# One 512-column product in place of two of 256 for the fourth form of a two-level scheme, and one more addition at the output

## The chip, the cores and the metric

The kernel runs on one core of a Trainium2 chip. The core has a matrix engine (TensorE, PE in the profile, with its weight loads as PEld), a vector engine (VectorE, DVE), an activation engine (ScalarE, ACT), GpSimd (POOL) and SyncE (SP), which here issues most of the DMAs. The metric is the device time of one execution in microseconds (us). Before the change the median of three runs is 686.04 us (685.83 to 686.23).

## The reference

An attention with 32 memory slots is followed by a feed-forward block with a gate.

```
a   = softmax(phi)                      # 8 batches, 8 heads, 576 positions, 32 slots
k_m = a^T k ;  v_m = a^T v              # 32 x 64 for each head
attn = softmax(q k_m^T / 8)
x   = (attn v_m), heads side by side    # 4608 x 512
h   = x w_in                            # 512 -> 2048
out = (h * sigmoid(h)) w_out            # 2048 -> 512
```

All arrays are float32.

## The kernel before, in words

The work goes batch by batch. For each batch the attention's probabilities `a` are made transposed, and `v_m` is folded into `w_in`, so that the hidden layer is one product of the probabilities with a projected weight. Numbers are held as a high and a low part in the type `F32R`, and a product of two numbers is three: high with high, high with low, low with high.

Batches 0 and 1 run plainly: 16 hidden chunks of 128 columns, each followed by `ffn2` (L712), which adds 512-column products into four PSUM banks, `acc`. During batch 1 the sums and differences of blocks of `w_out`, the forms of a Strassen-like scheme, are made (`w_forms`, L779) and kept: `kept[3j]`, `kept[3j+1]`, `kept[3j+2]` are the third, fourth and second form of step j. Each kept tile has 512 columns, the high part of the form in the first 256 and its low part in the last 256. `Q` is 256.

Batches 2 to 7 run the scheme. A batch has two halves of 256 main rows, `t` = 0 and 1, and a half has eight steps, `j` = 0 to 7 (`NP` is 8). Slot `s` of a batch issues, in this order: the 12 hidden products of step s (`ffn1s`, L818), the activation and the forms of the hidden values (`forms`, L836: the gate on ACT at L841, sums on DVE at L846, L849 and L850, high parts on ACT at L845 and L855, low parts on DVE at L856 and L857), the attention work planned for this slot, and then `st_step` (L875) for the step before it. `st_step` does seven products of a form of the hidden values with a form of the weights. Each is three products of 256 columns (`product`, L860): `HIGH` is high with high and high with low, `LOW` is low with high. They are added into four PSUM banks, `sums[0]` to `sums[3]`. A bank has 512 columns, and banks 0, 1 and 2 hold two blocks of 256, told apart by `place`. Bank 3 holds one, the fourth form's, in its first 256 columns; the other 256 columns are free. The first product into a bank after a new half begins sets it (`start`), and all later ones add.

In the order of a step, all `HIGH` products come first and then all `LOW` ones; the banks are met in the order 0, 3, 1, 2. The last step of a half mixes the two so that banks 0 and 3 are done early. After it, `st_out` (L896) combines the blocks: ACT copies banks 0 and 1, and the DVE does four additions (L910 to L913, all by the helper at L907): two read bank 2, one reads none, and the fourth subtracts bank 3 into `c21`. Then the stores of `c11` and `c21` are issued on SP (traced as L913 and L914). Three more additions are left to a later slot.

The four banks have one tag, `acc`, with four buffers. A new half's banks are given out by the planner from those that have been released; a bank is released when its last reader is done.

After batches 3, 5 and 7 the 64 leftover rows of two batches follow (`left_st`, L936), in three banks, `lsum`.

The order of PE and ACT instructions in this stage is the order of the program text. That of the DVE and of SP is the planner's, which at each point takes the earliest traced instruction that it finds ready.

Of the kernel before, what the change touches and what calls it, by code (L numbers as in the profile page):

```python
# [16 lines left out]
ALU = mybir.AluOpType  # L17
# [31 lines left out]
def attn_ffn_kernel(  # L49
# [708 lines left out]
    Q = DMODEL // 2  # L758
# [3 lines left out]
    kept, kept_at = [], []  # L762
# [97 lines left out]
    def product(bank, place, part, k, w, first):  # L860
        hi, lo = part
        whi, wlo = w
        for gt, wt in first:
            gt, wt = (hi, lo)[gt], (whi, wlo)[wt]
            key = bank, place
            nc.tensor.matmul(  # L866
                sums[bank][:, place * Q : (place + 1) * Q], gt[:, k], wt,
                start=bank not in begun, stop=True, skip_group_check=True,
            )
            begun.add(bank)  # L870

    sums, begun = [], set()
    HIGH, LOW = ((0, 0), (0, 1)), ((1, 0),)

    def st_step(b, t, j, part):  # L875
        if j == 0:
            sums[:] = [ps.tile([P, DMODEL], F32, tag="acc", name=f"sum{i}", bufs=NI) for i in range(4)]
            begun.clear()
        b11, b12, b21, b22 = (
            (wo_hi[:, 2 * j + k, q * Q : (q + 1) * Q], wo_lo[:, 2 * j + k, q * Q : (q + 1) * Q])  # L880
            for k in range(2) for q in range(2)
        )
        t3, t4, t2 = ((x[:, :Q], x[:, Q:]) for x in kept[3 * j : 3 * j + 3])
        todo = (
            (0, 0, 0, b11), (0, 1, 2, b21), (3, 0, 1, t4), (1, 0, 6, b22), (1, 1, 4, b12), (2, 0, 5, t2), (2, 1, 3, t3)
        )
        order = [(HIGH, todo), (LOW, todo)]
        if j == NP - 1:
            order = [(HIGH, todo[:5]), (LOW, todo[:2]), (HIGH, todo[5:]), (LOW, todo[2:])]
        for terms, some in order:  # L890
            for bank, place, k, w in some:
                product(bank, place, part, k, w, terms)
        if j == NP - 1:
            st_out(b, t)

    def st_out(b, t):  # L896
        o = sb.tile([P, 2, DMODEL], F32, tag="cva", name="oo", bufs=1)
        x = sb.tile([P, 2, Q], F32, tag="cva1", name="x", bufs=1)
        for i in range(2):
            nc.scalar.activation(o[:, i], sums[i], AF.Copy)  # L900
        (c11, c21), (p3, p5) = ((o[:, i, :Q], o[:, i, Q:]) for i in range(2))
        c12, c22 = x[:, 0], x[:, 1]
        r = b * S + 2 * t * P
        one, two = slice(r + P, r + 2 * P), slice(r, r + P)

        def add(to, a, c, op=ALU.add):
            nc.vector.tensor_tensor(to, a, c, op=op)  # L907

        add(c12, sums[2][:, :Q], c11)
        add(c22, sums[2][:, Q:], c12)  # L910
        add(c11, c11, c21)
        add(c21, c22, sums[3][:, :Q], ALU.subtract)
        nc.sync.dma_start(out[one, :Q], c11)  # L913
        nc.sync.dma_start(out[two, :Q], c21)  # L914

        def rest():
            add(c22, c22, p5)
            add(c12, c12, p5)
            add(c12, c12, p3)
            nc.sync.dma_start(out[two, Q:], c22)  # L920
            nc.sync.dma_start(out[one, Q:], c12)

        ev(*((b, 9) if t == 0 else (b, NFC + 1) if b % 2 else (b + 1, 3)), rest)
# [12 lines left out]
    def left_st(b, n, gs):  # L936
        if n == 0:
            sums[:] = [ps.tile([P, DMODEL], F32, tag="acc", name=f"lsum{i}", bufs=NI) for i in range(3)]
            begun.clear()
        part = [x.rearrange("p (n f) -> p n f", f=P) for x in gs]  # L940
        last = n == NLS - 1
        if last:
            o = sb.tile([P, DMODEL], F32, tag="cva", name="ol", bufs=1)
            x = sb.tile([P, Q], F32, tag="cva1", name="xl", bufs=1)
        for bank, (ks, q) in enumerate((((0,), 0), ((1,), 0), ((0, 1), 1))):
            cs = slice(q * Q, (q + 1) * Q)
            for i in range(2):
                for k in ks:
                    fc = 2 * (2 * n + i) + k
                    product(bank, 0, part, 2 * i + k, (wo_hi[:, fc, cs], wo_lo[:, fc, cs]), HIGH + LOW)  # L950
            if not last:
                continue
            if bank == 0:
                nc.scalar.activation(x, sums[0][:, :Q], AF.Copy)
                continue
            nc.vector.tensor_tensor(o[:, cs], sums[bank][:, :Q], x, op=ALU.add)
            for k, r in enumerate((b - 1, b)):
                queue = nc.scalar if b == B - 1 and k else nc.sync
                queue.dma_start(out[r * S + MAIN : r * S + S, cs], o[k * LEFT : (k + 1) * LEFT, cs])
# [3 lines left out]
    def ev(b, slot, fn, *a):  # L963
        events.setdefault((b, slot), []).append((fn, a))
# [40 lines left out]
    for b in range(B):  # L1005
        n = b + 1
# [183 lines left out]
    def finish(tiles):  # L1190
        if prev is None:
            return
        if prev[0] == "main":
            main_step(prev[1], prev[2], prev[3], tiles)
        elif prev[0] == "left" and tiles[0] == 0:
            if prev[1] < 2:
                left_step(prev[1], prev[2], prev[3])
                t1_load(prev[2])
            else:
                left_st(prev[1], prev[2], prev[3])  # L1200
        elif prev[0] == "st" and tiles[0] == 0:
            st_step(*prev[1:])
# [13 lines left out]
    for b in range(B):  # L1216
# [3 lines left out]
        for s in range(NFC if b > 1 else 0):  # L1220
            t, j = divmod(s, NP)
# [5 lines left out]
        for fc in range(NFC if b < 2 else 0):  # L1227
# [7 lines left out]
            for part in range(2):  # L1235
# [3 lines left out]
                n = len(traced)  # L1239
# [78 lines left out]
```

## Time and profile before

| What | Value |
|---|---|
| median of three runs | 686.04 us |
| profiled execution | 685.86 us |
| its span, first to last instruction | 684.0 us |
| PE busy | 673.9 us, 99% |
| PE weight loads busy | 595.7 us, 87% |
| DVE busy | 516.9 us, 76% |
| ACT busy | 368.3 us, 54% |
| products of L866 into `sum`, 256 columns | 2016 |
| granted TensorE clock | 1.000 |

A timeline row of the profile has the start in us from the span's beginning, the time from the first to the last instruction that it merges, the engine, the line, the operation, the tiles written and read, the shape and the count. Matrix products are pipelined: a product starts while the one before it is still on its way, so the busy time of one is a latency, and the distance between two starts is the pace. A weight load (PEld) runs ahead of its own product. In brackets stand the idle time of the engine just ahead, and what ended it.

### The profile page before, as it was taken

To read this page: it belongs to the slowest core of one execution; us is meant where nothing else is said; L and a number is where in the kernel's file an instruction comes from. 1 tells how busy PE (TensorE), PEld (TensorE's weight loads), DVE (VectorE), ACT (ScalarE), POOL (GpSimd) and SP (SyncE) were. 2 spreads that over 40 slices of the span, in tenths; PEclk is the share of its full clock that TensorE was granted. 3 is DMA by queue.
4 is the path that set the end of the run, shared out by engine and by line. 5 is a ranking of instruction groups with operands and counts; after the bars stand their busy time and mean duration, and the time that the engine had idled before them with its cause. 6 is when DMAs were issued, how large, how long until landed. Compare 5 with 4: busy or idle time off the path is not lost.

```text
span 684.0 us, 14812 instructions
## 1 busy us (share of the span) xinstructions
PE 673.9 (99%) x5932; PEld 595.7 (87%) x5932; DVE 516.9 (76%) x1087; ACT 368.3 (54%) x677; POOL 0.7 (0%) x6
## 2 busy tenths in 40 slices
PE   8899999999999999999999999999999999999997
PEld 3578778787889998899998999899989999889997
DVE  4897899988938588868876588886885668767653
ACT  3878684533535455644645546564653636554541
POOL 0000000000000000000000000000000000000000
PEclk9999999999999999999999999999999999999999
DMA  9998975224360562153420434125431204210001
GB/s 345 347 338 275 330 292 203 87 87 161 101 211 3 176 224 100 40 189 133 156 93 17 161 123 177 64 94 183 154 117 40 79 1 155 83 57 17 32 1 47
DMA packets 38228, 93.93 MB, mean 137 GB/s; under 512 B 4752, under 2 KB 22032, under 8 KB 34576
## 3 DMA queue, kind: packets, MB, share of 16 engines
q1 hardware_dynamic: 37136, 90.22, 37.9%
q10 hardware_dynamic: 1024, 2.77, 1.1%
q8 instruction: 47, 0.77, 0.4%
q14 instruction: 21, 0.17, 0.1%
HBM read 77.22 MB, written 15.73 MB: 136 GB/s over the span
## 4 chain that ended last, share of the span: by engine, by line
PE 74%; DVE 7%; ACT 2%; issue 2%; DMA 1%; SPq 1%; DVEq 0%; ACTq 0%
PE sum L866 32%; PE h L827 20%; PE acc L719 6%; PE lsum L866 5%; PE bg L636 3%; PE h L676 3%; PE accleft L719 2%; PE bg L335 1%; DVE pm L654 1%; PE bg L382 1%; DMA fm<-fm 1%; DVE gbuf L846 1%; SPq L88 1%; ACT gbuf L841 1%; DMA qz<-qm 1%
## 5 line engine op out<-in xcount | busy, mean ns | idle before, releaser
L827 PE MATMUL h<-aparts,pm 128*128 128x288 f32 x1152 | 169.1, 296 | 0.2 <-ACT gleft L843 0.2
L827 PEld LDWEIGHTS h<-aparts,pm 128*128 128x128 f32 x1152 | 157.0, 188 | 1.5 <-issue 0.7
L841 ACT ACTIVATE gbuf<-h 128x512 f32<-128x512 f32 x96 | 57.3, 596 | 124.5 <-PE h L827 122.6
L866 PE MATMUL sum<-wo_hi,aparts 128*128 128x256 f32 x384 | 104.0, 293 | 0.0
L866 PE MATMUL sum<-kept,aparts 128*128 128x256 f32 x576 | 100.1, 282 | 0.0
L866 PE MATMUL sum<-wo_lo,aparts 128*128 128x256 f32 x384 | 100.1, 282 | 0.0
L846 DVE TENSOR_TENSOR gbuf<-gbuf 128x256 f32<-128x256 f32 x96 | 40.5, 422 | 78.6 <-ACT gbuf L841 77.9
L866 PEld LDWEIGHTS sum<-wo_hi,aparts 128*128 128x128 f32 x384 | 72.8, 190 | 19.2 <-ACT gleft L843 15.9
L855 ACT ACTIVATE aparts<-gbuf 128x512 fp32r<-128x512 f32 x86 | 54.4, 633 | 64.4 <-DVE gbuf L850 64.4
L719 PE MATMUL acc<-wo_hi,gparts 128*128 128x512 f32 x256 | 85.3, 397 | 0.2
L866 PEld LDWEIGHTS sum<-kept,aparts 128*128 128x128 f32 x576 | 82.6, 191 | 0.0
L857 DVE TENSOR_TENSOR gparts<-gbuf,aparts 128x512 fp32r<-128x512 f32 x86 | 59.4, 690 | 18.5 <-ACT aparts L855 18.5
L866 PE MATMUL sum<-wo_hi,gparts 128*128 128x256 f32 x384 | 73.2, 281 | 0.0
L866 PEld LDWEIGHTS sum<-wo_lo,aparts 128*128 128x128 f32 x384 | 73.1, 190 | 0.0
L866 PE MATMUL sum<-kept,gparts 128*128 128x256 f32 x288 | 65.5, 282 | 0.0
L719 PEld LDWEIGHTS acc<-wo_hi,gparts 128*128 128x128 f32 x256 | 47.5, 188 | 14.5 <-DVE t L809 1.7
L866 PEld LDWEIGHTS sum<-wo_hi,gparts 128*128 128x128 f32 x384 | 59.4, 190 | 0.0
L676 PEld LDWEIGHTS h<-aparts,pm 128*128 128x128 f32 x372 | 51.8, 188 | 6.4 <-issue 1.8
L676 PE MATMUL h<-aparts,pm 128*128 128x288 f32 x372 | 56.0, 299 | 0.4 <-ACT aparts L604 0.4
L845 ACT ACTIVATE aparts<-gbuf 128x384 fp32r<-128x384 f32 x96 | 50.4, 525 | 0.0
L719 PE MATMUL acc<-wo_lo,gparts 128*128 128x512 f32 x128 | 49.4, 394 | 0.2 <-DVE wo_lo L182 0.2
L866 PEld LDWEIGHTS sum<-kept,gparts 128*128 128x128 f32 x288 | 47.9, 190 | 0.0
(206 smaller groups left out, 987.0 us busy)
## 6 DMA issues: line engine op xcount, KB each, us to landing
win<-win_saved SPq DMA_DIRECT2D x24, 1024.0 KB, 4.9
kv<-in_kv SPq DMA_DIRECT2D x28, 516.0 KB, 4.7
q<-in_q SPq DMA_DIRECT2D x16, 576.0 KB, 4.9
raw<-in_w_in SPq DMA_DIRECT2D x14, 512.0 KB, 7.8
raw<-in_w_out SPq DMA_DIRECT2D x6, 1024.0 KB, 5.9
win_saved<-win SPq DMA_DIRECT2D x4, 1024.0 KB, 8.7
phi<-in_phi SPq DMA_DIRECT2D x7, 576.0 KB, 5.9
out<-oo SPq DMA_DIRECT2D x26, 128.0 KB, 1.8
```

The source lines that it names most:

```text
L88: i = (queue or nc.sync).dma_start(dst, src)
L335: nc.tensor.matmul(pt[p][M * r : M * (r + 1), :KVW], e[:, p, c, M * r : M * (r + 1)], kvt[c][:, p, r], start=c == 0, stop=False, skip_grou ...
L636: nc.tensor.matmul(bg[M * r : M * (r + 1), p, :w].rearrange("p (k f) -> p k f", f=P), kvT[D * p : D * (p + 1), 1, r], src[D * p : D * (p + ...
L676: nc.tensor.matmul(h[:, hf, :HALF], wt[:, p, fs], a[:, p, hf * HALF : (hf + 1) * HALF], start=n[hf] == 0, stop=n[hf] == 5, skip_group_chec ...
L719: nc.tensor.matmul(acc[key], gt[:, cs], wt[:, fc], start=fc == 0 and n == 0, stop=fc == NFC - 1 and n == 2)
L827: nc.tensor.matmul(h[:, i, :HALF], wt[:, p, f : f + P], a[:, p], start=n == 0, stop=n == 5)
L841: nc.scalar.activation(gbuf[:, :MAIN].rearrange("p (i f) -> p i f", i=2), h[:, :, :w], AF.Silu)
L845: nc.scalar.activation(hi[:, :3], g[:, 1:4], AF.Copy)
L846: nc.vector.tensor_tensor(g[:, 4:6], g[:, :1].broadcast_to([P, 2, P]), g[:, 1:3], op=ALU.subtract)
L855: nc.scalar.activation(hi[:, 3:], g[:, 4:], AF.Copy)
L857: last_split.append(nc.vector.tensor_tensor(lo[:, 3:], g[:, 4:], hi[:, 3:], op=ALU.subtract))
L866: nc.tensor.matmul(sums[bank][:, place * Q : (place + 1) * Q], gt[:, k], wt, start=bank not in begun, stop=True, skip_group_check=True,)
```

## The change

For the fourth form (bank 3) the two `HIGH` products, with the form's high part and with its low part, become one product with the whole kept tile of 512 columns as its moving operand. It writes all 512 columns of bank 3: the product with the high part into the first 256, as before, and the product with the low part into the last 256. The `LOW` product of this form stays as it was, 256 columns into the first half. The two halves of the bank are added where the half batch ends: `st_out` has a fifth subtraction, which takes the last 256 columns of bank 3 from `c21`, behind the one that takes the first 256. The store of `c21` comes behind it.

```diff
@@ product
         for gt, wt in first:
+            if bank == 3 and (gt, wt) == (0, 1):
+                continue
             gt, wt = (hi, lo)[gt], (whi, wlo)[wt]
-            key = bank, place
+            n = wt.shape[-1]
             nc.tensor.matmul(
-                sums[bank][:, place * Q : (place + 1) * Q], gt[:, k], wt,
+                sums[bank][:, place * Q : place * Q + n], gt[:, k], wt,
                 start=bank not in begun, stop=True, skip_group_check=True,
             )
@@ st_step
             for bank, place, k, w in some:
+                if bank == 3 and terms is HIGH:
+                    w = (kept[3 * j + 1], None)
                 product(bank, place, part, k, w, terms)
@@ st_out
         add(c21, c22, sums[3][:, :Q], ALU.subtract)
+        add(c21, c21, sums[3][:, Q:], ALU.subtract)
         nc.sync.dma_start(out[one, :Q], c11)
```

## The prediction

> **What bounds the kernel now.** I read the page's busy shares first, then the chain that ended last, then a table by stages, and then the instructions in order of time around the lines that the change touches.
>
> ```profile
> span 684.0 us, 14812 instructions
> PE 673.9 (99%) x5932; PEld 595.7 (87%) x5932; DVE 516.9 (76%) x1087; ACT 368.3 (54%) x677; POOL 0.7 (0%) x6
> ...
> PE 74%; DVE 7%; ACT 2%; issue 2%; DMA 1%; SPq 1%; DVEq 0%; ACTq 0%
> PE sum L866 32%; PE h L827 20%; PE acc L719 6%; PE lsum L866 5%; PE bg L636 3%; PE h L676 3%; PE accleft L719 2%; PE bg L335 1%; DVE pm L654 1%; PE bg L382 1%; DMA fm<-fm 1%; DVE gbuf L846 1%; SPq L88 1%; ACT gbuf L841 1%; DMA qz<-qm 1%
> ```
>
> TensorE (PE) is busy 99% of the span, and the products of the changed function, PE sum L866, are alone 32% of the chain. The stage in which they run goes from about 204 us to the end, for batches 2 to 7:
>
> ```profile
> 204.00:684.00 480.00, 475.14 (x4434) 443.69 (x4418) 350.98 (x786) 249.64 (x481) 0.00 (x0) 1.00 0.29 97
> ```
>
> The columns are the stretch, its length, then busy us and count for PE, its weight loads, VectorE (DVE), ScalarE (ACT). PE has 475.14 of 480.00 us filled. So time taken from PE here comes off the end one for one, and so does time that PE is made to wait. A DVE instruction costs something only where PE waits for it.
>
> **The change, part by part.**
>
> *First, two products become one.* Each of the 96 steps (six batches, two halves, eight steps) loses one 256-column product with its weight load, and another grows to 512 columns. A busy time of 282 ns in the profile is a latency, not a pace; the pace is the distance between starts. A step has 21 products and then the 12 of the next hidden step. The rows of one step, with the DVE's and ACT's work beside it, which the second part needs too:
>
> ```profile
> 318.45 1.76 PE L827 MATMUL h<-aparts,pm 128*128 128x288 f32 x12
> ...
> 319.15 0.42 DVE L907 TENSOR_TENSOR x<-sum,oo 128x256 f32<-128x256 f32 x1
> 319.61 0.42 DVE L907 TENSOR_TENSOR x<-sum,x 128x256 f32<-128x256 f32 x1
> ...
> 319.95 0.41 DVE L907 TENSOR_TENSOR oo<-oo 128x256 f32<-128x256 f32 x1
> 320.05 0.28 PE L866 MATMUL sum<-wo_hi,aparts 128*128 128x256 f32 x1
> ...
> 320.24 0.60 ACT L841 ACTIVATE gbuf<-h 128x512 f32<-128x512 f32 x1 [0.76 <-PE h L827]
> ...
> 320.39 0.42 DVE L907 TENSOR_TENSOR oo<-x,sum 128x256 f32<-128x256 f32 x1
> ...
> 320.88 0.42 DVE L846 TENSOR_TENSOR gbuf<-gbuf 128x256 f32<-128x256 f32 x1
> ...
> 321.12 0.55 PEld L866 LDWEIGHTS sum<-kept,aparts 128*128 128x128 f32 x4
> ...
> 321.24 0.64 PE L866 MATMUL sum<-kept,aparts 128*128 128x256 f32 x4
> ...
> 322.54 1.22 PE L827 MATMUL h<-aparts,pm 128*128 128x288 f32 x8
> 322.65 0.69 DVE L857 TENSOR_TENSOR gparts<-gbuf,aparts 128x512 fp32r<-128x512 f32 x1 [0.23 <-ACT aparts L855]
> ```
>
> From 320.05 to 322.54 are 21 products: 2.49 / 21 = 0.1186 us each, so 0.237 for the pair that goes. For 512 columns the trace has the output products of an earlier stage, same type, same 128x128 weights; ten lie between these two starts, and twelve from the second pair on:
>
> ```profile
> 195.20 0.39 PE L719 MATMUL accleft<-wo_lo,gparts 128*128 128x512 f32 x1
> ...
> 197.47 0.40 PE L719 MATMUL accleft<-wo_hi,gparts 128*128 128x512 f32 x1
> ...
> 199.29 0.40 PE L719 MATMUL accleft<-wo_hi,aparts 128*128 128x512 f32 x1
> ...
> 202.05 0.43 PE L827 MATMUL h<-aparts,pm 128*128 128x288 f32 x2
> ```
>
> 2.27 / 10 = 0.227 us, and 2.76 / 12 = 0.230. I take 0.227: each step saves 0.237 - 0.227 = 0.010 us, and 96 of them 1.0 us. Starts are given to 0.01 us, so the difference is good to 0.002: 0.8 to 1.2 us; with 0.230 it is 0.7. The ends are 0.7 and 1.2.
>
> The Trainium skill (TensorE: Matmul & The Clock Gate, Back-to-back issue gap) gives the isolated gap of a warm product as its columns over 2.4 GHz plus about 2.5 ns. By it one product fewer is worth 2.5 ns, an estimate of 0.24 us over 96 steps. It speaks against the change; the same section's 131 ns for 512 columns in a stream speaks wildly for it. The starts above disagree with both (0.1186 and 0.227 us).
>
> *Second, one more subtraction where a half ends.* The new add (128x256, one operand in PSUM) runs 12 times, behind the subtraction that until now was the last reader of bank 3. Its price is that of its neighbours:
>
> ```profile
> L907 DVE TENSOR_TENSOR oo<-x,sum 128x256 f32<-128x256 f32 x12 | 5.0, 418 | 0.3
> ```
>
> That is 12 x 0.42 = 5 us of DVE time, which on its own hides beside PE. What does not hide is the bank. The four banks of a half are handed to the next half's four as they are read out: ACT frees two, then the DVE's second add one, and the subtraction (320.39, ends 320.81) the last. PE uses them in the order bank 0, 3, 1, 2, so the last freed goes to the eleventh product, the t2 form at 321.24 with its weight load at 321.12. That this product waits for that subtraction shows where it comes late:
>
> ```profile
> 443.46 0.28 PE L866 MATMUL sum<-wo_hi,aparts 128*128 128x256 f32 x1
> ...
> 443.67 0.60 ACT L841 ACTIVATE gbuf<-h 128x512 f32<-128x512 f32 x1 [0.94 <-PE h L827]
> ...
> 444.16 0.42 DVE L907 TENSOR_TENSOR oo<-x,sum 128x256 f32<-128x256 f32 x1
> ...
> 444.50 0.42 DVE L846 TENSOR_TENSOR gbuf<-gbuf 128x256 f32<-128x256 f32 x1
> 444.53 0.28 PE L866 MATMUL sum<-wo_lo,aparts 128*128 128x256 f32 x1
> ...
> 444.63 0.54 PEld L866 LDWEIGHTS sum<-kept,aparts 128*128 128x128 f32 x4
> 444.65 0.73 PE L866 MATMUL sum<-kept,aparts 128*128 128x256 f32 x4
> ```
>
> A weight load starts with the product before it; here it should be at 444.53, but it stands at 444.63, 0.05 after the subtraction ended (444.58), and the four products take 0.73 instead of 0.64. So the hand-over costs PE (end of the last read + 0.05) - (planned start of the eleventh product - 0.12), that is, end + 0.17 - planned start, where positive. At 320 us it is 320.81 + 0.17 - 321.24, free by 0.26 us.
>
> The new add needs the subtraction's result. Two dependent adds start 0.46 apart (319.15, 319.61), two independent ones 0.34 (319.61, 319.95). So the last read ends 0.46 later at best: 321.27. PE arrives 0.01 earlier, at 321.23: 321.27 + 0.17 - 321.23 = 0.21 us lost. This form stands at five hand-overs, from first to second half of batches 3 to 7; the last of them has the same 0.43 us between the read's end (639.91) and the product:
>
> ```profile
> 639.49 0.42 DVE L907 TENSOR_TENSOR oo<-x,sum 128x256 f32<-128x256 f32 x1
> ...
> 640.34 0.64 PE L866 MATMUL sum<-kept,aparts 128*128 128x256 f32 x4
> ```
>
> So 5 x 0.21 = 1.05 us.
>
> Four others. At 444 and 606 the DVE comes late from a projection (L654), and L846's input is ready (ACT L841 ends 444.27) while the subtraction runs. L846 is traced earlier than the adds and the DVE's order is the planner's, so I put L846 first, the add 0.34 behind it: start 444.84, end 445.26, + 0.17 - 444.64 = 0.79, less the 0.10 that is lost today: 0.69. At 606 it is 606.10 + 0.34 + 0.42 + 0.17 - 606.34 = 0.69:
>
> ```profile
> 605.76 0.42 DVE L907 TENSOR_TENSOR oo<-x,sum 128x256 f32<-128x256 f32 x1
> ...
> 606.10 0.42 DVE L846 TENSOR_TENSOR gbuf<-gbuf 128x256 f32<-128x256 f32 x1
> ...
> 606.35 0.64 PE L866 MATMUL sum<-kept,aparts 128*128 128x256 f32 x4
> ```
>
> ```profile
> 281.52 0.42 DVE L907 TENSOR_TENSOR oo<-x,sum 128x256 f32<-128x256 f32 x1
> ...
> 282.60 0.64 PE L866 MATMUL sum<-kept,aparts 128*128 128x256 f32 x4
> ```
>
> ```profile
> 243.78 0.41 DVE L907 TENSOR_TENSOR oo<-x,sum 128x256 f32<-128x256 f32 x1
> ...
> 244.12 0.28 DVE L849 TENSOR_TENSOR gbuf<-gbuf 128x128 f32<-128x128 f32 x1
> ...
> 245.00 0.64 PE L866 MATMUL sum<-kept,aparts 128*128 128x256 f32 x4
> ```
>
> At 281 the read ends at 282.40, 0.02 us in time: nothing. At 243 L846 already ran before the subtraction and L849 follows it; with the add behind L849 (244.45, end 244.87) 0.05 us is lost. The remaining three ends (second halves of batches 3, 5, 7) are followed by the leftover rows, which take three banks, those freed earlier: nothing, as the fourth bank is next wanted after four leftover steps. Behind the waiting product, PE's whole queue stands still, 10 more products and the next hidden step; nothing later on PE is free to run past it.
>
> On the DVE, the forms L846 to L857 move by up to 0.42 us. L857 ends 323.34; its result is read by the low products of the next step, which begins 1.60 us after 322.54 (12 hidden products, 318.45 to 320.05) and reads it after 13 to 14 of its own, at about 325.7. More than 2 us of cover is left. The store of the subtracted block leaves 0.46 us later; no row shows a wait on it.
>
> *The sum.* Saved 1.0; lost 1.05 + 0.69 + 0.69 + 0.05 = 2.5; net +1.5 us. The profiled execution took 685.86 us, 1.86 around its span of 684.0, so it would take 687.4. It lies 0.18 below the median of the runs shown, 686.04, on which the forecast is made: **687.5 us**.
>
> **The rivals.**
>
> *The add falls behind L846 at the five regular hand-overs too.* L846 began at 320.88, the add would be free to start at 320.85: a tie, which the planner settles before any run. Then the add runs 321.22 to 321.64, and each of the five loses 0.58: 2.9 + 1.4 + 0.05 - 1.0 = +3.3, 689.3 us. For it speaks the tie and 243 us, where L846 stands ahead of the subtraction; against it that L846 stands behind it at 320, 444 and 606.
>
> *The bank is free in time, and only the saving is left: 685.0 us.* One mechanism: the hand-over. It decides at 321.06 (321.23 - 0.17): if the planner gives the eleventh product a bank whose last read ends before that, or hands the late bank to no product of this step, none of the losses is there. Against it stands the late weight load at 444.63. For it: where slots go is the planner's choice, made with the new add in view.
>
> *The add is paid on the DVE's own path:* up to its 5 us in all, 691 us, if the shifted DVE work stalls the softmax or projections, whose stalls on PE exist today (DVE pm L654 is 1% of the chain). Against it: 2 us of cover above.
>
> *The removed product is worth next to nothing:* if the pace is set by columns alone, the saving is near 0.2 and the sum +2.3, 688.3 us. Against it are the two paces read above. By the skill's isolated gap it would come out so.
>
> **How the numbers follow.** The forecast has 0.45; L846 first 0.25; the saving alone 0.17; the DVE's own path 0.08; the worthless product 0.05. The forecast's own range is 686.9 to 687.9: the saving 0.7 to 1.2, and the adds at 444 and 606 directly behind the subtraction (0.47 each, not 0.69). Both signs hold chances, so the range goes from the saving alone to L846 first: 684.9 to 689.4; beyond it lie half of the saving-alone case and the DVE's path. A measurement tells 0.2%, 1.37 us, from no change: below 684.67 is faster, above 687.41 slower. Faster needs more than the saving's upper end: 0.05, taken from the saving-alone case for what the reads can miss. Same: the rest of that case and somewhat over half of the forecast, which lies on the limit: 0.38. Slower: the others, 0.57.
>
> **What would show it.** The 512-column product should take 0.226 to 0.230 from its start to the next. At the nine hand-overs the weight load of the eleventh product (now the tenth) should stand 0.05 after the new add ends, about 0.2 us late at five places and 0.5 to 0.7 at 444 and 606. Where L846 stands before or behind the add settles the first rival. The prediction is wrong if no weight load is late at those places, if PE's idle time appears elsewhere, or if paces outside the pair move.

## The result and the profile after

The changed kernel takes 687.35 us (median of 12 runs, 686.64 to 689.63); the kernel before, on the same chip, took 685.97 (12 runs). The ratio is 1.0024, with an interval of 1.0016 to 1.0031: slower by 1.4 us. The profiled execution took 687.2 us, with a span of 685.4 (before: 685.86 and 684.0).

From the page of the changed kernel, the span, the busy shares, the chain that ended last by engine and by line, and the two groups of products and weight loads that the change touches (busy us, mean ns of one, idle time ahead). The product's line is now L868, the additions' helper L911:

```profile
span 685.4 us, 14632 instructions
PE 674.6 (98%) x5836; PEld 591.2 (86%) x5836; DVE 520.8 (76%) x1099; ACT 368.2 (54%) x677; POOL 0.7 (0%) x6
...
PE 76%; DVE 7%; ACT 2%; issue 1%; DVEq 0%; ACTq 0%
PE sum L868 33%; PE h L827 20%; PE acc L719 6%; PE lsum L868 5%; PE bg L636 4%; PE h L676 3%; PE accleft L719 2%; PE bg L335 1%; DVE pm L654 1%; PE bg L382 1%; ACT pm L652 1%; DVE gparts L693 0%; ACT gbuf L841 0%; DVE oo L911 0%; DVE gbuf L846 0%
...
L868 PE MATMUL sum<-kept,aparts 128*128 128x256 f32 (+1 forms) x480 | 100.1, 306 | 0.4 <-DVE oo L911 0.4
...
L868 PEld LDWEIGHTS sum<-kept,aparts 128*128 128x128 f32 x480 | 70.7, 189 | 1.5 <-DVE oo L911 1.1
```

96 products are gone and 12 DVE additions have come. What is new is the releaser: products and weight loads of the `kept` forms now wait for `oo L911`, the additions. The 0.4 us in the first group is not what these waits cost. A product's busy time, 0.28 us, covers most of a hole in a stream that should start one every 0.12, so a late product shows as idle only when it is later than that. The loss must be read from starts.

The hand-over at 320 us, in time (start, length, engine, line, operation):

```profile
320.77 0.42 DVE L911 TENSOR_TENSOR oo<-x,sum 128x256 f32<-128x256 f32 x1
...
320.90 0.39 PE L868 MATMUL sum<-kept,aparts 128*128 128x512 f32 x1
...
321.13 0.28 PE L868 MATMUL sum<-wo_hi,aparts 128*128 128x256 f32 x1
...
321.23 0.42 DVE L911 TENSOR_TENSOR oo<-oo,sum 128x256 f32<-128x256 f32 x1
...
321.49 0.28 PE L868 MATMUL sum<-wo_lo,aparts 128*128 128x256 f32 x1
321.57 0.42 DVE L846 TENSOR_TENSOR gbuf<-gbuf 128x256 f32<-128x256 f32 x1
...
321.70 0.53 PEld L868 LDWEIGHTS sum<-kept,aparts 128*128 128x128 f32 x4
321.71 0.74 PE L868 MATMUL sum<-kept,aparts 128*128 128x256 f32 x4
```

The new addition (`oo<-oo,sum`) stands directly behind the subtraction, 0.46 us later, and ahead of L846. It ends at 321.65; 0.05 later the weight load of the tenth product starts. That product should have started at 321.61 (0.12 behind the one at 321.49) and starts at 321.71, and the four take 0.74 instead of 0.64: 0.20 us in all. The 512-column product goes 0.23 us to the next start.

The same at 444 and at 606 us, where the DVE comes late from a projection:

```profile
444.76 0.42 DVE L911 TENSOR_TENSOR oo<-oo,sum 128x256 f32<-128x256 f32 x1
444.77 0.28 PE L868 MATMUL sum<-wo_lo,aparts 128*128 128x256 f32 x1
445.10 0.42 DVE L846 TENSOR_TENSOR gbuf<-gbuf 128x256 f32<-128x256 f32 x1
...
445.23 0.53 PEld L868 LDWEIGHTS sum<-kept,aparts 128*128 128x128 f32 x4 [0.39 <-DVE oo L911]
445.23 0.62 PE L868 MATMUL sum<-kept,aparts 128*128 128x256 f32 x3 [0.18 <-DVE oo L911]
```

```profile
607.06 0.42 DVE L911 TENSOR_TENSOR oo<-oo,sum 128x256 f32<-128x256 f32 x1
607.07 0.28 PE L868 MATMUL sum<-wo_lo,aparts 128*128 128x256 f32 x1
...
607.53 0.74 PE L868 MATMUL sum<-kept,aparts 128*128 128x256 f32 x4 [0.18 <-DVE oo L911]
```

Here too the addition is ahead of L846 (at 606 us that one starts at 607.39), and the wait is long enough to be seen as idle time: 0.34 us from the planned 444.89 to 445.23, and 0.10 more as the loads have lost their lead. The kernel before lost 0.10 at the same place.

Each step from its first product to the first hidden product after it, in both traces, gives what a hand-over costs. Change of that length against before, in us, for the changed kernel and three of the experiments below:

```
hand-over (time before)   320    406    444    482    569    605    639    sum
changed kernel          0.206  0.204  0.343  0.205  0.198  0.431  0.204   1.79
addition alone          0.197  0.195  0.360  0.204  0.196  0.448  0.197   1.80
late bank used last    -0.009 -0.009 -0.098 -0.009 -0.009 -0.008 -0.009  -0.15
addition in two parts   0.259  0.273  0.411  0.266  0.271  0.510  0.259   2.25
```

At 243 and 281 us nothing is lost, and nothing at the ends of batches 3, 5 and 7. By the starts of the pair itself (0.2379 us in the mean before, 0.2331 for the 512-column product now) the merged product saves 0.0048 us a step, 0.47 us over the 96. The ordinary steps are shorter by 0.53 us in all, 0.006 in the mean, but 0.16 us are lost again in the stretches between the steps and behind the last, so that 0.37 us are left in this span.

Two more things stand between the spans. TensorE is 0.45 us later from about 10 us on, where it waits for a load (before, then after):

```profile
9.14 1.94 PE L335 MATMUL first<-kv,phi 128*32 128x129 f32 x54
```

```profile
10.41 0.65 PE L335 MATMUL first<-kv,phi 128*32 128x129 f32 x16 [0.46 <-DMA kv<-in_kv]
```

The same difference is 0.26 in another execution of the kernel before, and -0.15 to 0.44 in the experiments. And 0.44 us are won at 436: the step there is 0.34 shorter, and the hidden products behind it, whose first had to wait before, take 0.10 less. The kernel before, in order of time, and the issues of the small transfer `fm<-fm` from 424 to 430 us (count, KB, median us to landing):

```profile
430.04 0.29 DVE L303 COPY wide<-fm 128x256 f32<-128x256 f32 x1 [1.05 <-DMA fm<-fm]
...
436.47 1.32 PE L827 MATMUL h<-aparts,pm 128*128 128x288 f32 x8 [0.18 <-ACT gleft L843]
```

```profile
fm<-fm SPq DMA_DIRECT2D x3, 1.0 KB, 4.8
```

and after:

```profile
429.61 0.28 DVE L303 COPY wide<-fm 128x256 f32<-128x256 f32 x1
...
436.82 0.95 PE L827 MATMUL h<-aparts,pm 128*128 128x288 f32 x6
```

```profile
fm<-fm SPq DMA_DIRECT2D x3, 1.0 KB, 3.5
```

The transfer landed 1.3 us sooner, so the DVE doesn't wait for it and PE, six us later, not for ACT. The 0.10 that the kernel before lost at 444 goes with the same late transfer: it is there again in the second execution of that kernel, which has the wait too, and gone in the two experiments without that wait that leave the banks' last reads as they were (below: the merged product alone, and the operation that holds no bank). So the addition costs 1.79 + 0.10 = 1.89 us, the merged product saves 0.37, and the change itself makes 1.5. With the start (+0.45) and the transfer (-0.44 - 0.10) that is 1.43, the difference of the spans. Whether the early transfer is chance or belongs to the change isn't settled: if it belongs to it, the change makes only 1.0 in this span. The medians, 1.38 apart, can't tell.

### The profile page after: what moved, and what is told of

Read it like the earlier page. It is cut to its first block, busy times and chain, and to the rows that moved or that the text cites. A ratio compares the mean times of both kernels' runs of the same rounds, so it can differ in the third digit from the quotient of the medians.

```text
span 685.4 us, 14632 instructions
## 1 busy us (share of the span) xinstructions
PE 674.6 (98%) x5836; PEld 591.2 (86%) x5836; DVE 520.8 (76%) x1099; ACT 368.2 (54%) x677; POOL 0.7 (0%) x6
## 4 chain that ended last, share of the span: by engine, by line
PE 76%; DVE 7%; ACT 2%; issue 1%; DVEq 0%; ACTq 0%
PE sum L868 33%; PE h L827 20%; PE acc L719 6%; PE lsum L868 5%; PE bg L636 4%; PE h L676 3%; PE accleft L719 2%; PE bg L335 1%; DVE pm L654 1%; PE bg L382 1%; ACT pm L652 1%; DVE gparts L693 0%; ACT gbuf L841 0%; DVE oo L911 0%; DVE gbuf L846 0%
## 5 line engine op out<-in xcount | busy, mean ns | idle before, releaser
L868 PE MATMUL sum<-wo_hi,aparts 128*128 128x256 f32 x384 | 103.6, 292 | 0.0
L868 PE MATMUL sum<-kept,aparts 128*128 128x256 f32 (+1 forms) x480 | 100.1, 306 | 0.4 <-DVE oo L911 0.4
L868 PE MATMUL sum<-wo_lo,aparts 128*128 128x256 f32 x384 | 100.1, 283 | 0.0
L846 DVE TENSOR_TENSOR gbuf<-gbuf 128x256 f32<-128x256 f32 x96 | 40.5, 422 | 76.9 <-ACT gbuf L841 76.4
L868 PEld LDWEIGHTS sum<-wo_hi,aparts 128*128 128x128 f32 x384 | 72.6, 189 | 19.2 <-ACT gleft L843 15.9
L868 PEld LDWEIGHTS sum<-wo_lo,aparts 128*128 128x128 f32 x384 | 72.5, 189 | 4.1
L857 DVE TENSOR_TENSOR gparts<-gbuf,aparts 128x512 fp32r<-128x512 f32 x86 | 59.4, 691 | 18.6 <-ACT aparts L855 18.6
L868 PE MATMUL sum<-wo_hi,gparts 128*128 128x256 f32 x384 | 73.3, 282 | 0.0
L868 PEld LDWEIGHTS sum<-kept,aparts 128*128 128x128 f32 x480 | 70.7, 189 | 1.5 <-DVE oo L911 1.1
L868 PE MATMUL sum<-kept,gparts 128*128 128x256 f32 x288 | 65.6, 282 | 0.0
L868 PEld LDWEIGHTS sum<-wo_hi,gparts 128*128 128x128 f32 x384 | 59.2, 189 | 0.0
L868 PEld LDWEIGHTS sum<-kept,gparts 128*128 128x128 f32 x288 | 47.7, 189 | 0.0
```

Source lines behind the costliest of these rows:

```text
L846: nc.vector.tensor_tensor(g[:, 4:6], g[:, :1].broadcast_to([P, 2, P]), g[:, 1:3], op=ALU.subtract)
L857: last_split.append(nc.vector.tensor_tensor(lo[:, 3:], g[:, 4:], hi[:, 3:], op=ALU.subtract))
L868: nc.tensor.matmul(sums[bank][:, place * Q : place * Q + n], gt[:, k], wt, start=bank not in begun, stop=True, skip_group_check=True,)
```

## The experiments

The ratio is always that against runs of the kernel before on the same chip, 686.04 us for three of them (one more DVE operation, the DVE's load taken back, the weights elsewhere) and 685.78 for the other eight.

**The kernel before, once more.** No edit.

> The kernel before, unchanged, for a second profile and for how far one profiled execution lies from another. Theory and rivals alike: a ratio of 1.000 within 0.001. In the profile, PE waits a little in one half's hand-over (the t2 form's weight load at about 444 us is late by 0.10 us) and in no other; the time before the scheme's stage (to about 204.7 us) and the wait for a projection at about 436 us may differ by some tenths of a us, as they hang on where small DMAs land.

Measured: 685.94 us, 1.0002 (0.9994 to 1.0011), span 684.2. It is 0.26 us late from the start, and keeps 0.36 of the 0.44 at 436 us and the 0.10 at 444. So some 0.3 us of a single span is chance, and the differences of step lengths, good to about 0.01, carry the argument.

**The merged product alone.**

```diff
-        add(c21, c21, sums[3][:, Q:], ALU.subtract)
```

> The 512-column product without the fifth subtraction at the output: what the fourth form's high part with the weights' low part contributes is left out of the result. Theory (the pair is worth 96 times what its pace says; the profile after shows the 512-column product at 0.233 us against 0.238 for the pair): 0.5 us faster than before, 685.5, and no late weight load at the hand-overs but the one at 444 us. Rival 1 (the merged product itself is what costs, the addition is free): as slow as the changed kernel, +1.4. Rival 2 (the saving is the 1.0 us of the prediction): 685.0.

Measured: 685.17 us, 0.9992 (0.9984 to 1.0001), span 682.9. No weight load is late at a hand-over. The 96 products start 0.233 us before their successors (228 to 237 ns), as in the changed kernel: 0.47 us over the 96 again, and 0.37 left in the span. With the 0.54 of the transfer, which lands early here too, and 0.15 less at the start, that is 1.06, the difference of the spans; the medians show 0.61. So the saving exists, at about half its forecast; the ratio's interval alone just includes no change.

**The addition alone.** The two products stay apart and go into the two halves of bank 3.

```diff
+            at_ = 1 if bank == 3 and (gt, wt) == (0, 1) else place
...
-                sums[bank][:, place * Q : (place + 1) * Q], gt[:, k], wt,
+                sums[bank][:, at_ * Q : (at_ + 1) * Q], gt[:, k], wt,
...
+        add(c21, c21, sums[3][:, Q:], ALU.subtract)
```

> The fourth form's two high products stay two products of 256 columns, the one with the low weights written to the second half of bank 3, and the fifth subtraction is there: the result is whole. Theory (the addition holds the last bank 0.46 us longer): slower than before by what the nine hand-overs lose in the profile after, 5 x 0.20 + 0.34 + 0.43 = 1.8 us, 687.8, with late weight loads at the t2 form's first product in the same seven places. Rival 1 (the merged product costs): no change, 686.0. Rival 3 (the addition's 5 us of the vector engine are paid somewhere else than at the bank): slower, but with the weight loads in time.

Measured: 687.64 us, 1.0029 (1.0018 to 1.0040), span 685.8. The losses are those of the changed kernel (second row of the table: 1.80). In its order of time:

```profile
321.28 0.42 DVE L907 TENSOR_TENSOR oo<-oo,sum 128x256 f32<-128x256 f32 x1
...
321.75 0.54 PEld L866 LDWEIGHTS sum<-kept,aparts 128*128 128x128 f32 x4
```

End of the addition 321.70, weight load 0.05 behind it. The whole loss is the addition's, and the 512-column product has no part in it: 1.86 us from the medians here, 0.61 won in the run before, 1.25 together, against 1.38 for the whole change.

**The late bank used last.** The first step of a half meets banks 0, 3 and 1 with all their products, and bank 2's six products, those of the bank that is handed over last, come at its end.

```diff
+        if j == 0:
+            order = [(HIGH, todo[:5]), (LOW, todo[:5]), (HIGH, todo[5:]), (LOW, todo[5:])]
```

> The changed kernel, with the first step of each half in another order: the products of banks 0, 3 and 1, high and low, come ahead of all of bank 2, so that the last bank that is handed over is first met five products (0.6 us) later. Nothing is added or left out. Theory: the hand-over's loss, at most 0.54 us in one place, is gone, the 0.10 at 444 us too; what is left is the saving: 0.5 to 0.6 us faster than before, 685.4. Rival 3 (the addition is paid elsewhere on the vector engine): still slower than before by about 1.3 us, 687.3. Rival 4 (another bank's hand-over takes its place, that of bank 1, or low parts that are not ready): a wait at the sixth product or at the first low one, between the two.

Measured: 686.62 us, 1.0011 (1.0002 to 1.0020), span 684.4. The expectation missed. The bank is in time everywhere (third row of the table); at 444 us the weight load that waits for the addition's end at 445.16 would stand at 445.21, and it is wanted only at 445.35:

```profile
444.74 0.42 DVE L913 TENSOR_TENSOR oo<-oo,sum 128x256 f32<-128x256 f32 x1
...
445.35 0.55 PEld L868 LDWEIGHTS sum<-kept,aparts 128*128 128x128 f32 x4
```

But PE now waits elsewhere. Before, at the second projection of batch 3 (the products into `bg` at L636 wait for the DVE's split of the one before, L654, which reads that bank):

```profile
340.54 1.22 DVE L654 TENSOR_TENSOR pm<-bg,pm 128x1024 fp32r<-128x1024 f32 x1 [0.22 <-ACT pm L652]
...
341.84 0.18 PEld L636 LDWEIGHTS bg<-win,kvT 64*32 64x32 f32 x16 [0.17 <-DVE pm L654]
```

and with the late bank last:

```profile
341.11 1.23 DVE L654 TENSOR_TENSOR pm<-bg,pm 128x1024 fp32r<-128x1024 f32 x1 [0.22 <-ACT pm L652]
...
342.39 0.18 PEld L636 LDWEIGHTS bg<-win,kvT 64*32 64x32 f32 x16 [0.34 <-DVE pm L654]
```

The split is 0.57 us later, PE's own work only 0.38, and the idle time goes from 0.17 to 0.34. Five such places (342, 429, 454, 505 and 591 us; at 454 it is the products of L335 that go into the same bank) take 0.18, 0.19, 0.28, 0.18 and 0.07: 0.90 us together. That suggested a second price of the addition, its DVE time, which the next three kernels test.

**That order in the kernel before.**

```diff
+        if j == 0:
+            order = [(HIGH, todo[:5]), (LOW, todo[:5]), (HIGH, todo[5:]), (LOW, todo[5:])]
```

> The kernel before with only the other order of the first step of each half (banks 0, 3, 1 whole, then bank 2). Why the changed kernel with this order came out 0.84 us slower than before, where its hand-overs are all in time, is the question. Theory A (the addition's time on the vector engine: with PE no longer held at the bank, the projections' split, which PE needs, comes 0.18 to 0.25 us late, four to five times): here, without the addition, no such waits, and the 0.10 at 444 us gone: 685.7, ratio 0.9999. Theory B (the other order itself makes the waits): waits at the projections of 0.2 us each here too: slower than before by 0.7 us.

Measured: 685.94 us, 1.0004 (0.9995 to 1.0012), span 684.1. No new wait at any projection, and of the 0.10 at 444 only 0.02 is left. So the order costs nothing by itself.

**One more DVE operation that holds no bank.** In the kernel before, the maximum of c21 with itself behind the fourth subtraction.

```diff
         add(c21, c22, sums[3][:, :Q], ALU.subtract)
+        add(c21, c21, c21, ALU.max)
```

> The kernel before, with one more VectorE operation of the new addition's size right behind the fourth subtraction: the maximum of c21 with itself, which changes no value and reads no bank. So VectorE has the 0.42 us more in each half, and no bank is held longer. Theory (VectorE's own path): the banks are in time at every hand-over as before, and TensorE waits about 0.2 us more at a projection in batches 3 to 6, as with the late bank used last: plus 0.6 to 1.0 us, 686.4 to 686.8 us (ratio 1.001 to 1.0015). Rival (only the longer held bank costs anything): no change, ratio 1.000.

Measured: 686.49 us, 1.0007 (0.9998 to 1.0016), span 684.6. In order of time, the operation itself, the first product of the late bank (in time: four products in 0.64), and the projection 20 us later:

```profile
321.09 0.43 DVE L907 TENSOR_TENSOR oo<-oo 128x256 f32<-128x256 f32 x1
...
321.46 0.64 PE L866 MATMUL sum<-kept,aparts 128*128 128x256 f32 x4
...
340.98 1.22 DVE L654 TENSOR_TENSOR pm<-bg,pm 128x1024 fp32r<-128x1024 f32 x1 [0.22 <-ACT pm L652]
...
342.25 0.18 PEld L636 LDWEIGHTS bg<-win,kvT 64*32 64x32 f32 x16 [0.34 <-DVE pm L654]
```

The same five places lose 0.18, 0.19, 0.27, 0.19 and 0.08, 0.91 us, with no bank held, no merged product and no new order. Less the 0.54 of the transfer, which lands early here too, and with 0.24 more at the start, that is the 0.6 between the spans; the medians show 0.45. The ratio's interval alone just includes no change; the waits in the trace don't.

**The DVE's load taken back.** The kernel with the late bank last, without one of the deferred additions.

```diff
-            add(c12, c12, p3)
```

> The changed kernel with the late bank used last (as in the run with that order), and the deferred addition of p3 to c12 left out, so that one output block lacks the part p3. The VectorE work of a half is then back to its amount before the change; the saving and the order of the banks stay. Theory (VectorE is full from the end of a half to the splits of the projections, and 0.42 us more of it there costs TensorE about 0.2 us at a projection when it does not cost it at the bank): the waits of the projections' weight loads on the splits fall back to those of before, and only the saving is left, about 685.2 us (ratio 0.9985 to 0.9995). Part of them may stay if the deferred addition runs behind the splits in some halves. Rival (the waits come from the new order or from the 512-column product, not from VectorE's load): they stay, 0.07 to 0.25 us at five places, about 686.6 us (ratio 1.001).

Measured: 685.77 us, 0.9993 (0.9984 to 1.0001), span 684.3. The projections at 429, 505 and 591 us lose nothing any more; at 429:

```profile
427.89 1.23 DVE L654 TENSOR_TENSOR pm<-bg,pm 128x1024 fp32r<-128x1024 f32 x1 [0.22 <-ACT pm L652]
...
429.19 0.18 PEld L636 LDWEIGHTS bg<-win,kvT 64*32 64x32 f32 x16 [0.17 <-DVE pm L654]
```

At 454 the 0.27 stay: there the split comes 7 us after the hand-over, and no deferred addition lies between that could be left out. At 342 a new loss of 0.49 stands, of another kind, a small transfer that landed late:

```profile
338.51 0.20 DVE L296 TENSOR_REDUCE fm<-qz 32x8 f32<-32x32 f32 x1 [0.41 <-DMA qz<-qm]
```

No other kernel here shows an idle time at this place. So VectorE's load is the cause at three of the five places, shown by adding it (the run before this one) and by taking it back; at 454 by adding it alone.

**The addition in two parts of 128 columns.**

```diff
-        add(c21, c21, sums[3][:, Q:], ALU.subtract)
+        for n in range(2):
+            w = slice(n * P, (n + 1) * P)
+            add(c21[:, w], c21[:, w], sums[3][:, Q + n * P : Q + (n + 1) * P], ALU.subtract)
```

> The changed kernel with the fifth subtraction done as two of 128 columns, the suspected hold made longer. From the trace a 128-column add takes 0.29 us and two that don't depend on each other start 0.2 to 0.3 apart, so the last bank is let go 0.1 to 0.2 us later. Theory (the hand-over): slower than the changed kernel by 7 to 8 times that, about 1 us: 688.2 to 688.7, with the t2 form's weight load late by so much more at each of the seven places. Rival (the addition's place on the path is not the bank): no more than the vector engine's extra 0.15 us at a few places, within 0.3 us of the changed kernel.

Measured: 688.08 us, 1.0033 (1.0021 to 1.0046), span 686.1.

```profile
321.10 0.48 DVE L911 TENSOR_TENSOR oo<-oo,sum 128x128 f32<-128x128 f32 x2
...
321.64 0.53 PEld L868 LDWEIGHTS sum<-kept,aparts 128*128 128x128 f32 x4 [0.21 <-DVE oo L911]
```

The two take 0.48 us from first start to last end, 0.06 more than one of 256 columns, and each regular hand-over loses 0.06 more (0.26 against 0.20). The weight load again stands 0.06 behind the end (321.58). Loss follows the end of the last read one for one. At 281 us, where the changed kernel was in time by 0.02, 0.06 are lost too, and a projection at 505 waits 0.27 longer. The medians of the two kernels lie 0.73 apart, somewhat under the expected 1 us.

**The addition on GpSimd.** ACT copies the bank's second half out, into free columns, and GpSimd subtracts; the bank's last reader is then ACT or the fourth subtraction.

```diff
+        spare = aparts[:, :, 1, 2 * DMODEL : 2 * DMODEL + P]
+        nc.scalar.activation(spare, sums[3][:, Q:].rearrange("p (k f) -> p k f", k=2), AF.Copy)
...
-        add(c21, c21, sums[3][:, Q:], ALU.subtract)
+        c21k = c21.rearrange("p (k f) -> p k f", k=2)
+        nc.gpsimd.tensor_tensor(c21k, c21k, as_f32(spare), op=ALU.subtract)
```

> The changed kernel with the fifth subtraction taken off the vector engine: the scalar engine copies the second half of bank 3 (rounded to the matrix engine's type) right behind its two copies, and GpSimd, idle otherwise, subtracts that from the block before its store. Theory: bank 3 is let go with the vector engine's fourth addition as in the kernel before, so no new hand-over loss and no vector engine backlog; what is left is the saving of the merged product: 685.2, as in the run without the addition. The scalar engine's copy (0.4 us) stands where it is idle 0.7 to 0.9 us ahead of the gate, but at the first hand-over of batch 2 (243 us), where it may push the gate. Rival (the addition is not the cause, or GpSimd's work slows the vector engine): as slow as the changed kernel, 687.2.

Measured: 687.12 us, 1.0020 (1.0011 to 1.0029), span 685.2. A miss. The regular hand-overs are in time, and at 444 and 606 us only 0.07 is lost, but the DVE has not been relieved:

```profile
321.42 0.88 POOL L920 TENSOR_TENSOR oo<-oo,aparts 128x256 f32<-128x256 f32 x1 [38.25 <-DVE oo L913]
...
321.74 0.71 DVE L849 TENSOR_TENSOR gbuf<-gbuf 128x128 f32<-128x128 f32 x1
...
342.51 0.18 PEld L636 LDWEIGHTS bg<-win,kvT 64*32 64x32 f32 x16 [0.46 <-DVE pm L654]
```

L849, 0.29 us elsewhere, takes 0.71 beside GpSimd's subtraction and ends 0.15 after it. The DVE loses 0.42 us, what the addition itself would have taken, and the projections wait as above, and longer (0.29 at 342, 0.29 at 429, 0.57 at 505, 0.2 each at 291, 454 and 591). At 243 us 0.28 is lost as well: products there wait for ACT, which has the copy to do.

**GpSimd and the late bank last.** The edit before this one, and the order of banks.

> The kernel with the subtraction on GpSimd and, besides, the other order of the first step of each half. Theory: the 0.10 us at 444 goes too: 685.1, ratio 0.999. Rival (theory B of the run with the order alone): the projections wait as they did there.

Measured: 687.23 us, 1.0018 (1.0010 to 1.0027), span 685.6. The bank is in time at 444 and 606 as well; the waits at the projections stay. The bank was no longer the question.

**The weights of the 512-column product elsewhere.** The tiles that hold the high and the low parts of the forms change places.

```diff
-    form_low = [
+    form_high = [
...
-    form_high = [aparts[:, k, 1, :TF].rearrange("p (n f) -> p n f", f=P) for k in range(2)]
+    form_low = [aparts[:, k, 1, :TF].rearrange("p (n f) -> p n f", f=P) for k in range(2)]
```

> The changed kernel with the homes of the forms' high and low parts exchanged, so that the 512-column product reads its weights from gparts and not from aparts. If the pace of a 512-column product depends on where its weights lie, as the output products of the earlier stage suggest (0.227 us with gparts, 0.230 with aparts), the pace falls from 0.233 to about 0.227 us and the time by about 0.5 us. Rival (the pace is set by the company of the product, one of 512 columns between those of 256, not by the home): it stays at 0.233 us, and the time stays within 0.3 us of the changed kernel's.

Measured: 687.09 us, 1.0020 (1.0009 to 1.0031), span 685.2. The mean of the 96 distances is 0.233 us as before; the hand-overs lose the same. Where the weights lie is not what makes it slower than 0.227.

## Why the prediction was right or wrong

The forecast of 687.5 us stands 0.15 from the median, and its mechanism, the hand-over of the last bank, is what the runs show. Of its terms two were off, in opposite directions. The median lies on the forecast's own limit between no change (chance 0.38) and slower (0.57): it is 0.06 us under 687.41, but its ratio of 1.0024 is above the 0.2% that the limit was made from. So the choice between these two isn't put to the test.

**The saving: 1.0 forecast, 0.47 measured by the pair's starts, 0.37 left in the span.** The step that failed is "I take 0.227" for the 512-column product. In the changed kernel it takes 0.233 (changed kernel, merged product alone and exchanged homes alike), more than either row that I read in the earlier stage, 0.227 and 0.230, and more than the 0.226 to 0.230 that was named as a sign. The pair that goes was 0.238 by its own starts, near the 0.237 worked out. The difference of two nearly equal paces was the whole term, and one of them came from other company: there 512-column products follow each other, here one stands among products of 256. The rows read for the 0.230 had this in them: from 199.29 us the first six starts are 0.235, 0.231, 0.236, 0.228, 0.232 and 0.231 us apart and the next five 0.227, and a run with its weights in `gparts` (the twelve whose last starts at 176.57 us) begins in the same way. So 0.230 was the mean of a slow beginning and a steady pace, and a product that stands alone takes what the first ones take. Why a beginning is slower by some 6 ns isn't settled; the home of the weights is excluded. The Trainium skill (TensorE: Matmul & The Clock Gate, Back-to-back issue gap) would have made it 2.5 ns a step, an estimate of 0.24 us; the measured 5 ns lie between that and the 10 of my rows. For the product itself its formula gives 216 ns, against 233 here.

**The five regular hand-overs: 0.21 each forecast, 0.198 to 0.206 measured.** The rule, end of the last read + 0.17 - planned start, held: 321.65 + 0.17 - 321.61 = 0.21. The run with two parts moved the end by 0.06 and the loss by 0.06.

**444 and 606 us: 0.69 each forecast, 0.34 and 0.43 measured.** The step "I put L846 first" failed. The addition stands ahead of L846 at both, so the read ends at 445.18 and not 0.34 later. By the rule that is 445.18 + 0.17 - 444.89 = 0.46, the lower variant of 0.47 that the forecast's own range held; with the 0.10 that the late transfer had cost before, 0.44 was lost at 444. With this the rival that has L846 first everywhere fell as well; the tie at 320 went to the addition.

**243 and 281 us.** At 281 the forecast was in time by 0.02:

```profile
282.40 0.42 DVE L911 TENSOR_TENSOR oo<-oo,sum 128x256 f32<-128x256 f32 x1
...
283.01 0.40 PE L868 MATMUL sum<-kept,aparts 128*128 128x256 f32 x2
```

282.82 + 0.17 = 282.99, and the product starts at 283.01, on time. At 243 the order was as forecast (L846, subtraction, L849, addition), but the addition began 0.20 behind L849 and not 0.33, and the 0.05 were not lost:

```profile
244.55 0.28 DVE L849 TENSOR_TENSOR gbuf<-gbuf 128x128 f32<-128x128 f32 x1
244.75 0.41 DVE L911 TENSOR_TENSOR oo<-oo,sum 128x256 f32<-128x256 f32 x1
...
245.43 0.64 PE L868 MATMUL sum<-kept,aparts 128*128 128x256 f32 x4
```

**The sum.** Saved 0.37 in place of 1.0, lost 1.89 in place of 2.5: +1.5, as forecast, and 1.38 between the medians. Both sides were put 0.6 us too high; that the total came so near is luck, while the five regular hand-overs, half of the loss, came as worked out.

**The DVE's own path.** I held it covered by 2 us, and gave it a chance only for more than the banks cost. The cover was read at the wrong consumer. L857's result does have that time, but the same DVE goes on from there to the splits of the projections (L654), and there only some 0.2 us were free: 0.42 us more of DVE work takes 0.2 from PE at a projection (0.9 us over five places with the maximum that holds no bank). In the changed kernel this isn't seen, because PE has already been held up 0.2 us at the bank:

```profile
341.12 1.23 DVE L654 TENSOR_TENSOR pm<-bg,pm 128x1024 fp32r<-128x1024 f32 x1 [0.22 <-ACT pm L652]
...
342.42 0.18 PEld L636 LDWEIGHTS bg<-win,kvT 64*32 64x32 f32 x16 [0.16 <-DVE pm L654]
```

Split and projection are both 0.58 us later than before, and the wait between them is unchanged. So the two prices are not added, the first hides the second. This is also why no repair of the bank gave the saving alone: with the bank in time, 0.90 us appear at the projections.

**The other rivals.** "The bank is free in time" did not happen, the planner still gives the tenth product the bank read last; and its time of 685.0 would not have followed from that alone, as the kernel with the late bank last (686.62) shows. "The removed product is worth next to nothing" was half true.

## What to carry to other kernels

A new reader of a bank is priced where the bank is handed on: the end of the last read plus what it takes to get the weight load and its product going (0.17 us here), against the start that PE had planned, at each hand-over by itself. When an engine off the critical path is filled from one meeting point to the next, find all the points at which the critical engine meets it and the slack at each; an added operation is paid at the first one that has too little, and curing that one moves the payment to the next. A gain that is the small difference of two paces has to be read in the company in which the product will run.

## What was unexpected of the hardware

GpSimd is no free help to VectorE. Its subtraction of 128x256 took 0.88 us at 321 us (GpSimd's spans in the profile are rough), twice VectorE's 0.42, and a VectorE subtraction of 128x128 beside it took 0.71 us in place of 0.29 and ended 0.15 after GpSimd's. The Trainium skill (SBUF — State Buffer, Who interferes with whom) says that a VectorE instruction with two inputs in SBUF contends with a GpSimd instruction that reads SBUF. The trace agrees: L849 reads twice from `gbuf`, and it is as long beside GpSimd at each of the six other hand-overs where the two overlap (0.70 to 0.72 us). Whether it stood still or ran slowly the trace doesn't show.

A late weight load costs PE a second time: behind the late product the next one starts 0.22 us later and not 0.12 (0.74 for four products, against 0.64). At 321 us the late load starts at 321.704 and its product at 321.706, the next load at 321.812 and its product at 321.926; in time, a load starts 0.12 ahead of its product.

The landing time of a transfer of 1 KB, 3.2 to 4.8 us after its issue, decided 0.44 us of PE's time at 436 us. It is issued 1.2 to 1.5 us behind a load of 1 MB on the same queue, and the first of the three lands 1.5 to 1.6 us behind that load in the three executions of kernels that have neither the merged product nor more DVE work, and 0.2 to 0.3 behind it in the ten others; why isn't settled.
